# Causal attention and routed experts on one core: transposes in 64-row halves, shared columns for diagonal blocks, one ring of PSUM banks

## The chip, the core and the metric

The kernel runs on one core of a Trainium2 chip. The metric is the device time of one execution in microseconds; the time before is the median of three runs. Engines: TensorE (PE; its weight loads are listed as PEld), VectorE (DVE), ScalarE (ACT), GpSimd (POOL), and SyncE (SP), whose queue issues most DMA transfers.

## What is computed

A causal attention over 4 sequences of 448 tokens with 12 heads of 64, then a layer of 8 experts, each of which takes its 224 best tokens in one greedy order over all (token, expert) scores.

```python
def _attn_ref(q, k, v):                       # (4, 12, 448, 64)
    scores = scale * np.matmul(q, k.transpose(0, 1, 3, 2))
    scores = np.where(mask, -1000000000.0, scores)   # mask: above the diagonal
    scores = scores - np.max(scores, axis=-1, keepdims=True)
    attn = np.exp(scores)
    attn = attn / (np.sum(attn, axis=-1, keepdims=True) + 1e-09)
    return np.matmul(attn, v)

def _moe_ref(x, w_gate, w1, w2):              # x: (1792, 768), 8 experts
    order = np.argsort(-(x @ w_gate).flatten())
    ...                                       # a token goes to its first expert that still has room (224)
    for e in range(E):
        h = np.maximum(x[assigned == e] @ w1[e], 0.0)
        out[assigned == e] = h @ w2[e]
```

## The kernel before

The kernel has two stages. Attention (class Attention, the first 164 us or so) works on 24 pairs of heads; a pair's two heads sit in the lower and the upper 64 partitions. Routing and experts (classes Router and Experts) follow. In each stage a planner (class Schedule) puts every operation in order at build time: each operation is a task with an engine, a guessed duration, dependencies and a priority, and the planner walks through time and lets each engine take the ready task of highest priority. Some copies may go to ScalarE or VectorE, whichever the planner finds free. TensorE is the exception: its tasks hang on one another in the order in which they are added (`pe`, line 454).

That order is set in `plan` (line 434). In turn n TensorE does the scores of pair n in two sets (query blocks 2 and 3, then 1 and 0), the values of pair n-2, the transposes of P of pair n-1, the rows of pair n-3, and, when a set of four pairs is complete, the logits.

A pair goes through these steps. `scores` multiplies the four query blocks of 128 rows (the first and last 64 tokens share one block) with as many keys as the mask leaves (QM: 192, 320, 448 and 64 columns), each head in its own half of the array's rows and in its own PSUM bank. `mask` (VectorE) adds the mask and finds the row maximum, `exp` (ScalarE) writes the exponentials to a tile P and their sums. `transp` turns the 16 blocks of P of 128 x 128, one instruction each, four to a bank: groups 0 and 1 hold one head's blocks, group 2 blocks of both, group 3 the diagonal blocks of 64 keys, each of which holds both heads' in its two halves. `keep_pt` copies them to the tile PT: groups 0 and 1 with 512 columns on ScalarE, group 2 with 512 columns on either engine, group 3 as two copies of 64 partitions x 256 columns, one for each head. PT has a half for each head; the places that the causal mask leaves empty were set to zero once at the start. `av` multiplies four key blocks of V (448, 320, 192 and 64 query columns) with it, each head in its own half of the array's columns, and `xt_ev` evicts the result. For the first 12 pairs (LATE) `rows_tr` and `rows_dve` turn the result back to token rows and scale it by the sums; the later pairs' rows are turned after attention.

PSUM has eight banks. Four belong to the ring "s" (scores), four to the ring "t" (everything else): the dependency `ring(name, n)` makes a task wait until the bank that it will write has been emptied.

Of the kernel before, what the change touches and what calls it, by code (L numbers as in the profile page):

```python
# [30 lines left out]
KO = (256, 704, 64, 0)  # L31
KM = (448, 320, 192, 64)
XO = (0, 64, 192, 320)
LATE = 12
# [126 lines left out]
class Attention(Schedule):  # L161
    def __init__(self, ctx, tc, gc, keep, k, qk, vP, wgP, xd, L):
# [17 lines left out]
        t = self.ps.tile([P, 512], F32, name="t", bufs=4)  # L180
# [14 lines left out]
        self.PTs = [self.cs.tile([P, 2, 1024], F32, name=f"PT{z}") for z in range(2)]  # L195
        for t in self.PTs:
            for sd, o in ((sd, o) for sd in range(2) for o in (0, 640)):
                nc.gpsimd.memset(t[64 - 64 * sd:128 - 64 * sd, sd, o:o + 128], 0.0)


# [17 lines left out]
    def load_v(self, g):  # L218
        v = self.ld.tile([P, 4, NC, D], F32, name="v")
        b, h = divmod(4 * g, H)  # L220
        self.nc.sync.dma_start(v, self.vP[:, b, h:h + 4])
        for u in range(4):
            self.V[4 * g + u] = v[:, u]

    def scores(self, pp, lst):
        ts = [self.ps.tile([P, 512], F32, name="s", bufs=4) for _ in range(2)]
# [53 lines left out]
    def keep_pt(self, e, pp, c):  # L280
        PT = self.PTs[pp % 2]
        if c < 2:
            self.copy(e, PT[:, c, 128:640], self.T[pp, c])
        elif c == 2:
            self.copy(e, PT[:, :, 768:], self.T[pp, 2].rearrange("p (s k) -> p s k", s=2))
        else:
            sd = c - 3
            h = slice(64 * sd, 64 * sd + 64)
            self.copy(e, PT.rearrange("p s (c z k) -> p s c z k", z=2, k=64)[h, sd, 0:6:5],
                      self.T[pp, 3][h].rearrange("p (c z y k) -> p c z y k", c=2, z=2, y=2)[:, :, :, 1])  # L290
# [65 lines left out]
    def logits_mm(self, p0, m):  # L356
        t = self.ps.tile([128, S], F32, name="t", bufs=4)
# [4 lines left out]
    def logits_direct(self, pp):  # L362
        b, q = divmod(pp, 6)
        if q == 4:
            self.u[pp] = self.ps.tile([P, NC, 128], F32, name="t", bufs=4)
# [9 lines left out]
    def logits_tr(self, p0, m):  # L375
        u = self.u[p0] = self.ps.tile([P, NC, 128], F32, name="t", bufs=4)
# [33 lines left out]
    def ring(self, name, n):  # L410
        r = self.rings.setdefault(name, [])
        return r[-n] if len(r) >= n else []

    def plan(self, rt):
        add = self.add
        self.rings = {}
# [41 lines left out]
    def score_set(self, pp, lst):  # L458
# [11 lines left out]
        a = self.pe(m * 4 / 2400.0 + 0.01 * len(lst), work, [self.got[pp]] + self.ring("s", 2), 1)  # L470
        free = []
        for sd in range(2):
            for i in lst:
# [5 lines left out]
        self.rings.setdefault("s", []).append(free)  # L479
# [4 lines left out]
    def turns(self, pp):  # L484
# [3 lines left out]
        every = [(sd, i) for sd in range(2) for i in range(NC)]  # L488
# [844 lines left out]
```

## Time and profile before

| | before |
|---|---|
| median of three runs | 486.27 us (484.93 to 487.37) |
| profiled execution | 486.56 us, span 484.9 us |
| instructions | 10216 |
| TensorE busy | 471.2 us (97%) |
| TensorE weight loads | 398.3 us (82%) |
| VectorE busy | 376.7 us (78%) |
| ScalarE busy | 298.9 us (62%) |
| granted TensorE clock, mean | 0.999 |

The shares are means over a stage of attention and a stage of experts that have different limits, so the windows by stage have to be read beside them. A matmul's end is modelled and matmuls overlap in the pipeline: the step from one start to the next is what one costs, not its listed duration. Of an fp32 product each instruction of the program is two loads and two matmuls in the trace; a transpose is one of each.

### The profile page before, as it was taken

Reading aid. Unit: us, or ns where it says so; the run is one execution under the profiler, and the core shown is the slowest. Engines: PE = TensorE matmul, PEld = TensorE weight load, DVE = VectorE, ACT = ScalarE, POOL = GpSimd, SP = SyncE. Lnnn points to the kernel's source line nnn. Section 1 sums busy time; section 2 is a strip of 40 time slices with the busy share of each in tenths; the row PEclk is TensorE's granted clock in tenths of the full one; section 3 lists DMA queues with packets and bytes.
Section 4 is the critical chain, followed back from the end, with each engine's and each line's share of the span. In section 5 each row is a group of like instructions: output and inputs, shape, how many; then the busy total and the mean of one; then the engine's idle time right before and its main releaser. Section 6 shows DMA issues by size and latency. Waiting matters only on the chain.

```text
span 484.9 us, 10216 instructions
## 1 busy us (share of the span) xinstructions
PE 471.2 (97%) x3697; PEld 398.3 (82%) x3697; DVE 376.7 (78%) x1316; ACT 298.9 (62%) x759; POOL 52.6 (11%) x100
## 2 busy tenths in 40 slices
PE   8999999999999898999989999999999999999994
PEld 4767777676766767998979999989899989999994
DVE  4988788897788675799989999999999585684510
ACT  4997988889989542345654664572763673764410
POOL 7000000000000110100310300300114110301001
PEclk9999999999999999999999999999999999999999
DMA  8633183172000078497577677764955886681101
GB/s 288 268 120 120 44 310 120 45 263 91 1 2 2 23 236 286 142 334 245 181 248 258 198 215 243 245 193 134 321 197 183 315 271 216 220 245 64 53 1 57
DMA packets 19187, 84.84 MB, mean 175 GB/s; under 512 B 2240, under 2 KB 4928, under 8 KB 19136
## 3 DMA queue, kind: packets, MB, share of 16 engines
q1 hardware_dynamic: 16464, 73.14, 44.5%
q0 software_dynamic: 2672, 11.04, 7.3%
q8 instruction: 29, 0.48, 0.4%
q14 instruction: 22, 0.18, 0.1%
HBM read 73.16 MB, written 11.01 MB: 174 GB/s over the span
## 4 chain that ended last, share of the span: by engine, by line
PE 77%; DVE 11%; ACT 5%; DMA 4%; issue 2%; POOL 1%; POOLq 0%; DVEq 0%; ACTq 0%
PE po L1258 23%; PE ph L1224 10%; PE s L233 9%; PE t L297 9%; PE t L268 8%; PE ph L1228 5%; DVE wl L1154 4%; PE ph L1219 3%; ACT P L254 3%; DMA xio<-xd,idx 2%; DVE G L697 2%; PE ph L1189 2%; PE rt L798 2%; DMA out<-xio,idx 1%; PE po L1219 1%
## 5 line engine op out<-in xcount | busy, mean ns | idle before, releaser
L1154 DVE TENSOR_TENSOR wl<-wr,wh 128x512 fp32r<-128x512 f32 x180 | 116.2, 682 | 13.5 <-ACT wh L1148 13.5
L1148 ACT CAST wh<-wr 128x1536 fp32r<-128x1536 f32 x60 | 88.9, 1482 | 59.9 <-DMA wr<-in_w 38.8
L1224 PE MATMUL ph<-xhl,wh 128*128 128x448 f32 x336 | 109.2, 380 | 0.0
L254 ACT ACTIVATE P<-Sm,mx 128x448 f32<-128x448 f32 (+2 forms) x192 | 95.7, 504 | 19.9 <-DVE mx L244 19.8
L1228 PE MATMUL ph<-xhl,wl 128*128 128x224 f32 x336 | 88.8, 264 | 0.0
L1258 PE MATMUL po<-wh,HH 128*112 128x384 f32 x256 | 68.2, 342 | 0.0
L1258 PE MATMUL po<-wh,HL 128*112 128x384 f32 x256 | 67.9, 341 | 0.0
L1258 PE MATMUL po<-wl,HH 128*112 128x384 f32 x256 | 67.3, 339 | 0.0
L1224 PEld LDWEIGHTS ph<-xhl,wh 128*128 128x128 f32 x336 | 63.1, 188 | 5.1 <-issue 0.6
L1228 PEld LDWEIGHTS ph<-xhl,wl 128*128 128x128 f32 x336 | 64.1, 191 | 0.0
L233 PE MATMUL s<-raw 64*128 64x448 f32 (+3 forms) x384 | 51.8, 404 | 0.3 <-DVE mx L244 0.2
L233 PEld LDWEIGHTS s<-raw 64*128 64x128 f32 x384 | 31.9, 187 | 20.7 <-issue 15.7
L268 PE MATMUL t<-idf,P 128*128 128x128 f32 x384 | 47.7, 277 | 0.0
L297 PE MATMUL t<-PT,v 128*64 128x448 f32 (+3 forms) x384 | 46.8, 386 | 0.0
L297 PEld LDWEIGHTS t<-PT,v 128*64 128x64 f32 x384 | 25.4, 136 | 23.8 <-issue 14.0
L1258 PEld LDWEIGHTS po<-wl,HH 128*112 128x112 f32 x256 | 44.0, 175 | 0.3
L268 PEld LDWEIGHTS t<-idf,P 128*128 128x128 f32 x384 | 41.5, 140 | 2.3 <-ACT P L254 0.4
L1258 PEld LDWEIGHTS po<-wh,HL 128*112 128x112 f32 x256 | 43.2, 175 | 0.3
L1258 PEld LDWEIGHTS po<-wh,HH 128*112 128x112 f32 x256 | 43.1, 175 | 0.3
L274 DVE COPY PT<-t 64x256 f32<-64x256 f32 (+1 forms) x56 | 29.6, 529 | 16.3 <-PE t L268 10.5
L244 DVE CUSTOM_DVE_ANT_0 Sm<-s,MK 128x448 f32<-128x448 f32 (+2 forms) x72 | 33.2, 486 | 9.5 <-PE s L233 8.8
L244 DVE CUSTOM_DVE_ANT_0 Sm<-s,MR 128x64 f32<-128x64 f32 (+3 forms) x120 | 40.5, 380 | 0.0
(170 smaller groups left out, 617.1 us busy)
## 6 DMA issues: line engine op xcount, KB each, us to landing
wr<-in_w SPq DMA_DIRECT2D x64, 768.0 KB, 5.1
raw<-in_qk SPq DMA_DIRECT2D x11, 896.0 KB, 8.9
v<-in_v SPq DMA_DIRECT2D x12, 512.0 KB, 4.5
xd<-xio SPq DMA_DIRECT2D x2, 1152.0 KB, 5.0
xd<-xio SPq DMA_DIRECT2D x3, 576.0 KB, 4.3
xd<-xio SPq DMA_DIRECT2D x3, 192.0 KB, 5.2
raw<-in_qk SPq DMA_DIRECT2D x1, 448.0 KB, 4.3
xd<-xio SPq DMA_DIRECT2D x1, 384.0 KB, 4.2
```

The source lines that it names most:

```text
L233: self.nc.tensor.matmul(ts[sd][:, o:o + m], q[:, 0, QS[i]:QS[i] + P], k, start=True, stop=True)
L244: self.nc.vector.tensor_tensor_reduce(Sm[:, QO[i] + sd * m:QO[i] + sd * m + m], self.S.pop((pp, sd, i)), mk, -0.125, 3.0e38, OP.add, OP.mi ...
L254: self.nc.scalar.activation(X[:, s], Sm[:, s], AF.Exp, bias=mx[:, sd, i:i + 1], scale=-1.0, accum_out=self.RS[b][:, pr, sd * NC + i:sd * N ...
L268: self.nc.tensor.transpose(t[:, n * P:n * P + P], X[:, o:o + P], idf)
L274: self.nc.vector.tensor_copy(out, x)
L297: self.nc.tensor.matmul(self.AV[pp][sd * 64:sd * 64 + 64, XO[j]:XO[j] + KM[j]], self.V[2 * pp + sd][:, j, :], self.PTs[pp % 2][:, sd, KO[j ...
L1148: self.nc.scalar.copy(hi, self.R[p, c])
L1154: self.nc.vector.tensor_sub(lo[:, s], self.R[p, c][:, s], hi[:, s].bitcast(F32))
L1219: nc.tensor.matmul(t[:, c], self.R[p, f // 2][:, s], self.X[0, 0][:, d, 0, c], start=d == 0, stop=d == 5)
L1224: nc.tensor.matmul(t[:, :2 * CAP], hi[:, s], x[:, d].rearrange("p z t -> p (z t)"), start=d == 0, stop=False)
L1228: nc.tensor.matmul(t[:, :CAP], lo[:, s], x[:, d, 0], start=False, stop=d == 5)
L1258: self.nc.tensor.matmul(self.T[p, "o", u][z][:, :384], a[p][:, f, u * C:u * C + C], w[:, o:o + 384], start=f == 0 and n == 0, stop=f == 7 ...
```

## The change

A block of P is now turned as two halves of 64 rows: 64 x 128 weights from the lower or the upper partitions against a 64 x 64 identity. The lower half goes to one bank, the upper half to another, side by side in 64 columns each. The copies to PT (`keep_pt(e, pp, g, z)`) put them together again with a target of 64-element runs. Of the four diagonal blocks only the upper halves are turned, and the two heads share their columns in PT: V gets three more blocks per head (7 instead of 4), padded with zeros in the half that belongs to the other head, and `av` does seven products a head instead of four, over 384, 256, 128 and four times 64 columns. PT is an ordinary tile of 2048 columns with two buffers, and nothing in it is set to zero beforehand. The rows of the first 12 pairs are turned two pairs at a time, in halves as well, into two banks, and scaled with one operation for each head (`rows_two`). All banks of attention come from one ring of eight in the order of their use (`bank`, `room`). The planner's guesses change with it: scores, transposes and rows count as one mode.

```diff
-KO = (256, 704, 64, 0)
-KM = (448, 320, 192, 64)
-XO = (0, 64, 192, 320)
+KR = (384, 256, 128)
+DJ = (2, 1, 3, 0)
...
+    def bank(self):
+        return self.ps.tile([P, 512], F32, name="s", bufs=8)
...
-        v = self.ld.tile([P, 4, NC, D], F32, name="v")
+        v = self.ld.tile([P, 4, 2 * NC - 1, D], F32, name="v")
...
     def transp(self, pp, g):
-        t = self.T[pp, g] = self.ps.tile([P, 512], F32, name="t", bufs=4)
-        if g < 2:
-            parts = [(g, 2, 2)] + [(g, i, 0) for i in range(3)]
-        elif g == 2:
-            parts = [(sd, i, 1) for sd in range(2) for i in (1, 2)]
+        t = self.T[pp, g] = [self.bank() for _ in range(2)]
+        if g == 0:
+            parts = [(sd, i, j) for sd in range(2) for i, j in ((0, 0), (1, 0), (2, 0), (2, 2))]
         else:
-            parts = [(None, i, 0) for i in (2, 1, 3, 0)]
+            parts = [(sd, i, 1) for sd in range(2) for i in (1, 2)] + [(None, i, 0) for i in DJ]
         for n, (sd, i, j) in enumerate(parts):
             o = QO[i] + (QM[i] - 64 if sd is None else QM[i] + 64 + (i - j) * P if sd else j * P)
-            self.nc.tensor.transpose(t[:, n * P:n * P + P], X[:, o:o + P], idf)
+            for z in range(sd is None, 2):
+                h = slice(64 * z, 64 * z + 64)
+                self.nc.tensor.transpose(t[z][:, n * 64:n * 64 + 64], X[h, o:o + P], idf[h, h])
...
+    def keep_pt(self, e, pp, g, z):
+        if pp not in self.PT:
+            self.PT[pp] = self.wk.tile([P, 2048], F32, name="PT", bufs=2)
+        n = 256 if g > z else 512
+        x = self.PT[pp][:, g * 1024:g * 1024 + 2 * n].rearrange("p (c z k) -> p c z k", z=2, k=64)[:, :, z]
+        self.copy(e, x, self.T[pp, g][z][:, :n].rearrange("p (c k) -> p c k", k=64))
 
     def av(self, pp, js):
         if 0 in js:
-            self.AV[pp] = self.ps.tile([P, 512], F32, name="t", bufs=4)
+            self.AV[pp] = self.bank()
+        PT = self.PT[pp]
         for j in js:
             for sd in range(2):
-                self.nc.tensor.matmul(self.AV[pp][sd * 64:sd * 64 + 64, XO[j]:XO[j] + KM[j]], self.V[2 * pp + sd][:, j, :],
-                                      self.PTs[pp % 2][:, sd, KO[j]:KO[j] + KM[j]], start=j == 0, stop=j == 3)
+                v = self.V[2 * pp + sd]
+                o = (512 * sd, 1024 + 256 * sd, 512 * sd + 384)[j] if j < 3 else 1600 + 128 * (j - 3)
+                w, m = (384 - KR[j], KR[j]) if j < 3 else ((320, 192, 384, 64)[j - 3], 64)
+                self.nc.tensor.matmul(self.AV[pp][sd * 64:sd * 64 + 64, w:w + m],
+                                      v[:, j if j < 3 else 3 + (3, 2, 0, 1)[j - 3], :], PT[:, o:o + m],
+                                      start=j == 0, stop=j == 6)
...
     def rows_tr(self, pp):
-        self.T[pp] = self.ps.tile([P, 512], F32, name="t", bufs=4)
-        self.rows_mm(pp, self.T[pp])
+        self.T[pp] = [self.bank() for _ in range(2)]
+        for u, i, sd in ((u, i, sd) for u in range(2) for i in range(NC) for sd in range(2)):
+            h = slice(64 * sd, 64 * sd + 64)
+            o = u * 256 + i * 64
+            self.nc.tensor.transpose(self.T[pp][sd][:, o:o + 64], self.block(self.XT[pp - 1 + u][h], i), self.k["idf"][h, h])
...
-    def ring(self, name, n):
-        r = self.rings.setdefault(name, [])
-        return r[-n] if len(r) >= n else []
+    def room(self, n):
+        o = len(self.ring) - 8
+        return sum(self.ring[max(o, 0):max(o + n, 0)], [])
...
-        for g, need in ((3, every), (0, every), (1, every), (2, every)):
-            a = self.pe(0.44, lambda g=g: self.transp(pp, g), [self.exps[pp, sd, i] for sd, i in need] + self.ring("t", 4))
...
+        for g in range(2):
+            a = self.pe(0.51, lambda g=g: self.transp(pp, g), every + self.room(2), 1)
+            for z in range(2):
+                dur = {"DVE": 0.6, "ACT": 0.47} if g <= z else {"DVE": 0.35, "ACT": 0.29}
+                c = self.add("ACT" if g == 0 else "ACT/DVE", dur["ACT"] if g == 0 else dur,
+                             lambda e="ACT", g=g, z=z: self.keep_pt(e, pp, g, z), [a] + self.avs[-2:-1], pr + 0.3)
+                self.pts[pp, g, z] = c
+                self.ring.append([c])
...
-        for js, cs in (((0,), (0, 1, 3, 4)), ((1, 2, 3), (2,))):
+        for js, g in (((0, 2), 0), ((1, 3, 4, 5, 6), 1)):
```

## Rows read from the trace of the kernel before

**Rows 1.** Windows by stage: busy us (instructions) of each engine, PEclk, DMA share, GB/s.
```profile
8.00:26.00 18.00, 17.68 (x134) 12.28 (x134) 16.01 (x82) 17.96 (x67) 2.26 (x9) 1.00 0.76 288
26.00:104.80 78.80, 78.79 (x659) 55.62 (x658) 65.99 (x278) 68.06 (x234) 0.45 (x3) 1.00 0.37 131
104.80:148.20 43.40, 43.40 (x363) 29.83 (x362) 35.74 (x154) 40.03 (x139) 0.00 (x0) 1.00 0.18 65
148.20:164.00 15.80, 15.34 (x130) 10.54 (x130) 11.39 (x52) 9.73 (x32) 1.76 (x4) 1.00 0.01 2
```

**Rows 2.** Chain of waits in order of time: start, us, what; attention.
```profile
26.01 2.04 PE s L233 x16
...
52.14 0.44 PE t L324 x4
...
104.81 2.04 PE s L233 x16
106.85 1.88 PE t L297 x16
108.73 1.90 PE t L268 x16
...
148.17 2.04 PE s L233 x16
```

**Rows 3.** Groups by form, 26 to 104.8 us (count, busy, mean ns, idle); last 8 to 26.
```profile
L254 ACT ACTIVATE P<-Sm,mx 128x448 f32<-128x448 f32 x24 | 15.9, 662 | 10.2 <-DVE mx L244 10.2
L272 ACT COPY PT<-t 128x512 f32<-128x512 f32 x24 | 12.9, 583 | 0.0
L274 DVE COPY PT<-t 64x256 f32<-64x256 f32 x18 | 7.6, 423 | 5.7 <-PE t L268 2.8 <-ACT PT L272 2.8
L272 ACT COPY PT<-t 64x256 f32<-64x256 f32 x6 | 2.2, 365 | 0.2
...
L272 ACT COPY PT<-t 64x256 f32<-64x256 f32 x4 | 1.4, 358 | 0.0
```

**Rows 4.** Weight loads of one pair's transposes: timeline at 96 us, group of the page.
```profile
96.15 1.73 PEld L268 LDWEIGHTS t<-idf,P 128*128 128x128 f32 x16
...
L268 PEld LDWEIGHTS t<-idf,P 128*128 128x128 f32 x384 | 41.5, 140 | 2.3 <-ACT P L254 0.4
```

**Rows 5.** Four transposes of 64 rows: timeline at 158.7 us, min/median/max of line 378.
```profile
158.73 0.33 PEld L378 LDWEIGHTS t<-idf,lt 64*128 64x128 f32 x4 [0.17 <-issue]
158.73 0.46 PE L378 MATMUL t<-idf,lt 64*128 64x64 f32 x4
...
L378 PEld LDWEIGHTS t<-idf,lt x24: 137/140/142, 45.6 to 158.9; 128*128 128x128 f32 x20, 64*128 64x128 f32 x4
L378 PE MATMUL t<-idf,lt x24: 222/273/275, 45.7 to 159.0; 128*128 128x128 f32 x20, 64*128 64x64 f32 x4
```

**Rows 6.** Scores, two heads in two row halves: timeline at 99 us, group by form.
```profile
98.92 0.30 PEld L233 LDWEIGHTS s<-raw 64*128 64x128 f32 x4 [0.17 <-issue]
99.41 0.19 PEld L233 LDWEIGHTS s<-raw 64*128 64x128 f32 x2 [0.18 <-issue]
...
100.70 0.33 PE L233 MATMUL s<-raw 64*128 64x192 f32 x2
...
L233 PE MATMUL s<-raw 64*128 64x192 f32 x48 | 5.9, 322 | 0.0
```

**Rows 7.** Window of the early count, line 726 alone: PE, PEld, PEclk, DMA, GB/s.
```profile
163.64:163.89 0.25, 0.25 (x10) 0.25 (x10) 1.00 0.00 0
```

**Rows 8.** Values in 64 columns: timeline at 102.6 us, groups by form.
```profile
102.63 0.28 PE L297 MATMUL t<-PT,v 128*64 128x64 f32 x4
...
L297 PEld LDWEIGHTS t<-PT,v 128*64 128x64 f32 x192 | 12.7, 136 | 11.7 <-issue 6.9 <-ACT P L254 1.1 <-DVE mx L244 0.2
...
L297 PE MATMUL t<-PT,v 128*64 128x64 f32 x48 | 3.4, 220 | 0.0
```

**Rows 9.** Timeline of TensorE at 13 us: end of pair 0's transposes, scores of pair 2.
```profile
13.09 0.38 PE L268 MATMUL t<-idf,P 128*128 128x128 f32 x2
13.40 0.65 PE L233 MATMUL s<-raw 64*128 64x448 f32 x2
```

More of the change, by code (lines that the diff above doesn't have):

```diff
@@ L179, in __init__ @@
         nc.vector.memset(zero, 0.0)
[L180 removed]
+        t = self.bank()
         for _ in range(WARM):
@@ L225, in scores @@
     def scores(self, pp, lst):
-        ts = [self.ps.tile([P, 512], F32, name="s", bufs=4) for _ in range(2)]
+        ts = [self.bank() for _ in range(2)]
         o = 0
@@ L468, in work @@
                 self.fire(self.qfree[pp])
-        a = self.pe(m * 4 / 2400.0 + 0.01 * len(lst), work, [self.got[pp]] + self.ring("s", 2), 1)
-        free = []
+        a = self.pe(m * 4 / 2400.0 + 0.01 * len(lst), work, [self.got[pp]] + self.room(2), 1)
         for sd in range(2):
+            free = []
             for i in lst:
@@ L478, in score_set @@
                                            [d], pr + early)
-        self.rings.setdefault("s", []).append(free)
+            self.ring.append(free)
         if last:
@@ L487, in turns @@
         pr = 5.5 - 0.1 * pp
-        every = [(sd, i) for sd in range(2) for i in range(NC)]
-        for g, need in ((3, every), (0, every), (1, every), (2, every)):
-            a = self.pe(0.44, lambda g=g: self.transp(pp, g), [self.exps[pp, sd, i] for sd, i in need] + self.ring("t", 4))
-            last = [a]
-            for c in (3, 4) if g == 3 else (g,):
-                dur = {"DVE": 0.61, "ACT": 0.49} if c < 3 else {"DVE": 0.35, "ACT": 0.27}
-                one = c < 2
-                up = 0.6 if c > 2 else 0.3
-                last = [self.add("ACT" if one else "ACT/DVE", dur["ACT"] if one else dur,
-                                 lambda e="ACT", c=c: self.keep_pt(e, pp, c), last + self.ring("av", 2), pr + up)]
-                self.pts[pp, c] = last[0]
-            self.rings.setdefault("t", []).append(last)
+        every = [self.exps[pp, sd, i] for sd in range(2) for i in range(NC)]
+        for g in range(2):
[6 more added lines that the diff above has]
+                self.ring.append([c])
     def values(self, pp):
@@ L504, in values @@
         pr = 5.5 - 0.1 * pp
-        for js, cs in (((0,), (0, 1, 3, 4)), ((1, 2, 3), (2,))):
-            m = sum(KM[j] for j in js)
+        for js, g in (((0, 2), 0), ((1, 3, 4, 5, 6), 1)):
+            m = sum((384, 256, 128, 64, 64, 64, 64)[j] for j in js)
             def work(js=js):
                 self.av(pp, js)
-                if 2 in js and pp in self.vfree:
+                if 1 in js and pp in self.vfree:
                     self.fire(self.vfree[pp])
-            deps = [self.pts[pp, c] for c in cs] + [self.gotv[pp // 2]]
-            a = self.pe(m * 4 / 2400.0 + 0.02, work, deps + (self.ring("t", 4) if 0 in js else []), 2)
-        self.rings.setdefault("av", []).append([a])
+            deps = [self.pts[pp, g, z] for z in range(2)] + [self.gotv[pp // 2]]
+            a = self.pe(m * 4 / 2400.0 + 0.02, work, deps + (self.room(1) if 0 in js else []), 2)
+        self.avs.append(a)
         def ev(e):
@@ L531, in rows_at @@
         pr = 5.3 - 0.1 * pp
[L532 to L535 removed]
+        t = self.pe(0.5, lambda: self.rows_tr(pp), [self.xts[pp]] + self.room(2), 1)
+        for sd in range(2):
+            d = self.add("DVE", 0.62, lambda sd=sd: self.rows_two(pp, sd), [t, self.rec[pp]], pr + 0.3)
+            self.ring.append([d])
+            self.done_x.append(d)
         if b < LATE // 6:
@@ L544, in logits @@
         if pp in (NP - 2, NP - 1):
-            free = self.ring("t", 4) if q == 4 else []
+            free = self.room(1) if q == 4 else []
             self.lts = self.pe(0.4, lambda: self.logits_direct(pp), [self.xts[pp]] + free)
             if q == 4:
-                self.rings.setdefault("t", []).append([self.event(0.0)])
+                self.ring.append([])
             return
```

51 lines of the change are left out of this document (20 added, 31 removed).

## Prediction

> **What bounds the kernel now.** I read the stage windows first [rows 1]. From 26 us to 148 us TensorE is busy in 78.79 of 78.80 us and 43.40 of 43.40 us, ScalarE in 86% and 92%, VectorE in 84% and 82%, at a granted clock of 1.00. From 8 to 26 us it is the other way round: ScalarE is busy in 17.96 of 18.00 us. The chain of waits [rows 2] says the same: from 26.01 us it runs through TensorE alone, sixteen scores, sixteen value matmuls, sixteen transposes, then scores again, with nothing between. So inside the attention stage a pair of heads costs what TensorE needs for it: (104.81 - 26.01)/12 = 6.57 us while rows are turned in the stage, (148.17 - 104.81)/7 = 6.19 us after that, made of 2.04 + 1.88 + 1.90, rows 0.44, and a rest of some 0.35 that is logits, once in four pairs. From 148.2 us the tail of the last two pairs runs to about 164 us; what follows is routing and experts, which the change doesn't touch, so what attention saves comes off the end one for one. The groups by form [rows 3] price each operation of the stage; ScalarE's 10.2 us of idle there are waits for masks, that is, for scores that TensorE delivers late.
>
> **The change part by part, TensorE.** Transposes of P: 16 instructions of 128 rows become 28 of 64 rows. They come as 12 pairs (lower and upper half of a block, into two banks) and 4 upper halves alone, so 16 steps if the two of a pair run together. Price now: 16 loads in 1.73 us of which the last takes 0.14, so 15 steps of 0.106 [rows 4]; the chain charges 1.90 for all, up to the next scores [rows 2]. Price of a step with 64 rows and 64 columns: the kernel has four such transposes, alone, in its second to last logits set: four loads in 0.33 us with a last of 0.14, three steps of 0.063; four matmuls in 0.46 with a last of 0.22, 0.24 for three steps, so 0.05 more at the entry [rows 5]. New price 16 x 0.063 + 0.05 = 1.06, a saving of 0.84 a pair.
>
> That a pair runs in one step isn't shown for transposes, but the scores are the same shape of work (64 x 128 weights in either half of the rows, two banks): two loads take 0.19 us from the first one's start to the last one's end and four 0.30, so two and two start together, 0.11 apart; two matmuls of 0.322 are over in 0.33 [rows 6]. Bounds for 28 instructions: 12 + 4 steps of 0.063 (1.06), or 28 steps of 0.063 one after the other (1.81). I take the first, since the row of the scores is the nearest. Issuing doesn't limit it: ten small matmuls, each with its load, begin within 0.25 us, 0.028 apart [rows 7], and a step here has two such pairs in 0.063.
>
> For a rule against it: the Trainium skill, "TensorE: Matmul & The Clock Gate", section "LDWEIGHTS (loading the stationary operand)", says that a load's time goes by its columns, at P/1.2 ns, however few rows it fills, so that half the rows cost as much as all, 107 ns for 128 columns. By that the 28 loads would take 28 x 0.107 = 3.0 us if they followed one another. The 0.063 of [rows 5] are 128 columns in less than that, so the trace does not agree.
>
> Rows: four transposes a pair (0.44) become sixteen halves for two pairs, 8 steps x 0.063 = 0.50, 0.25 a pair: -0.19 in the pairs with rows. Scores: their first loads now come 0.17 us late behind the 128-row transposes [rows 6]. After transposes of the same 64-row shape that wait should go, except in the one pair of four where a logits matmul lies between; part of it is already in the 1.90, so I take -0.08 (between 0 and -0.17). Values: 16 instructions become 28, with the same 1024 columns a head; four blocks of 64 stand where one of 448 and one of 64 gave 512. A 64-column step takes 0.06 [rows 8] (four in 0.28, a last of 0.22), eight are 0.48, and 512 columns at the present rate (1.88/2048 of a column pass) are 0.47: +0.02. Upper bound, if the load of 0.136 [rows 8] isn't hidden behind a 64-column pass: 8 x 0.076 = +0.6.
>
> Sum: 6.57 - 0.84 - 0.19 - 0.08 + 0.02 = 5.48 us with rows, 6.19 - 0.84 - 0.08 + 0.02 = 5.29 without.
>
> **VectorE and ScalarE, the cover that is gone.** They now work 65.99 + 68.06 = 134.05 us in twelve pairs, 11.17 a pair, and 35.74 + 40.03 in seven, 10.82 [rows 1]. The change takes away the two 64 x 256 copies of a pair (7.6 + 2.2 us in twelve pairs, 0.82 a pair) and puts one 128 x 256 copy there, whose length along the free axis is that of one of them, 0.42 on VectorE, 0.36 on ScalarE [rows 3]: -0.41. The three 512-column copies stay, two tied to ScalarE as before; their target in runs of 64 elements I cost at nothing (no copy of before has such a target; at worst it adds what a second instruction adds over one of half the length: two copies of 256 columns take 2 x 0.36 for ScalarE's 0.58 in one, +0.14 each, 0.2 us a pair for either engine). Rows on VectorE: two of 512 columns for two pairs, as now. So 10.76 and 10.41 a pair: 5.38 and 5.21 for each engine if the planner could share perfectly. That is level with TensorE's 5.48 and 5.29. All three engines would reach their limit at once, so I don't expect TensorE's whole gain to show.
>
> The Trainium skill, "TensorEngine Tiling (Array Packing)", section "PSUM Bottleneck", says that splitting the array speeds TensorE and not the emptying of PSUM, which may become the limit. Here the busy sums of [rows 1] bear it out at 5.4 us a pair.
>
> How near do two engines come to full? From 8 to 26 us, when TensorE didn't hold them back, they worked 16.01 + 17.96 of 36 us, 94% [rows 1]. I take 10.76/2/0.944 = 5.70 and 10.41/2/0.944 = 5.51 us a pair; bounds are TensorE's 5.48 and 5.29, and 88% (today's mean of 85 to 87% a little bettered), 6.1 and 5.9.
>
> **What else moves.** Start: ScalarE bounds it, and four of its copies of 64 x 256 (1.4 us in 8 to 26 [rows 3]) become at most two to four of 128 x 256 that VectorE may take: -0.8. Tail (148.2 to 164): two more blocks of transposes, each 0.84 shorter [rows 2]: -1.7. Loads: each v transfer grows from 512 to 896 KB. The first one stands ahead of the queries and keys of pairs 2 and 3 on SyncE's queue; 384 KB at the 288 GB/s of 8 to 26 us [rows 1] delay those by 1.3 us. Pair 2's scores start at 13.40 [rows 9], behind transposes and not behind a load, and ScalarE is at work without a gap then; so I take 0, at most 1.3. Later loads have four buffers of lead. The zeroing of the old PT tiles on GpSimd goes, at nothing either way.
>
> Ring: 8 banks in one order instead of 4 + 4, with the same 10.5 banks a pair. A bank of scores must now be emptied before a later transpose can write, and after a rows step the first scores of a pair need the last masks of the pair before, the second ones the copies of its first transposes. Behind such a scores matmul on TensorE stand the values and transposes, and behind its result the masks and exponentials. Cost 0 if VectorE does the masks before other work and the copies leave at once; otherwise it is the second rival below.
>
> **Sum of the forecast**: 12 x (6.57 - 5.70) = 10.4, 7 x (6.19 - 5.51) = 4.8, 0.8, 1.7: 17.7 us. The profiled execution took 486.56 us (span 484.9), 0.3 above the median of the three runs, 486.27. So 469.
>
> **Rivals.**
> A, TensorE's whole gain is had: 12 x 1.09 + 7 x 0.90 + 2.5 = 21.9, 464 to 465. For it: the shares are close. Against: three engines that share a pair through strict orders, where even now two idle 8 to 18%.
> B, the ring and the copies take the place of the transposes: a copy of the first transposes waits behind one exponential (0.66) and then takes two times 0.58, so the second scores, due 1.0 us into a pair, would start up to 0.6 late in pairs with rows, half that in others: 5.48 + 0.6 = 6.1 and 5.29 + 0.3 = 5.6 to 5.85 us, some 10.5 saved in all, about 476, and with copies behind two exponentials 480.
> C, the two halves of a pair run one after the other at 0.063: turns 1.81, rows 0.50 a pair: 6.57 - 0.09 + 0.06 - 0.08 + 0.02 = 6.48 and 6.04; 1.1 + 1.0 + 0.8 + 0.2 = 3.1 saved, 483.5.
> D, slower: the halves run one after the other and each costs a whole step, about 0.109, as a 128-row transpose does (the chain's 1.90 over 16 less the entry [rows 2]). Place: the transposes of P and rows. Turns 28 x 0.109 = 3.05 (+1.15 in 24 pairs), rows 1.74 for two pairs (+0.86 six times), scores -0.08 x 24: +27.6 + 5.2 - 1.9 = +31, 517. It decides from (1.90 + 0.08)/28 = 0.071 an instruction on, and [rows 5] show 0.063. The rule of the Trainium skill cited above ("TensorE: Matmul & The Clock Gate", loads) gives this same end.
> E, the gain is lost later (constants for routing that VectorE does in its free time slip behind attention, the values' loads aren't hidden): 484 to 488.
>
> **How the numbers follow.** Forecast (88 to 98% of the two engines, 465 to 476) 0.64; A 0.08 (462 to 465); B beyond 476 0.12; C 0.05; D 0.05; E 0.06. The range 462 to 480 leaves out C, D, E and a little of A and B, under 2 in 10. About 0.5% (2.4 us) is what a measurement of this kernel can tell from no change. Faster: forecast, A, B and most of C, 0.87. Same: E's better part and a rest of C, 0.06. Slower: D and E's rest, 0.07.
>
> **What would show it.** Transposes right: TensorE's sixteen-step block in about 1.06 us with two loads starting together; wrong: starts 0.06 or 0.11 apart for every instruction. Bound right: in the window of the twelve pairs ScalarE and VectorE over 92% busy, TensorE at 92 to 97%, a chain of waits that goes through exponentials and PT copies; A if TensorE is still without a gap; B if scores wait for PT copies or masks for over 0.3 us a pair. Tail and experts: the same length after the last values. The prediction is wrong if pairs stay over 6.1 us, or if a lower granted clock shows in the stage.

## The result and the profile after

The changed kernel takes 469.35 us (median of four runs, 468.12 to 472.33) against 485.71 of the kernel before on the same chip: a ratio of 0.9668, 95% interval 0.9613 to 0.9722. On a second chip it took 469.6, ratio 0.9676 (0.9606 to 0.9747). The forecast was 469.0, the range 462 to 480.

| | after |
|---|---|
| median of four runs | 469.35 us (468.12 to 472.33) |
| profiled execution | 468.12 us, span 466.4 us |
| instructions | 11432 |
| TensorE busy | 450.0 us (96%) |
| TensorE weight loads | 392.9 us (84%) |
| VectorE busy | 367.6 us (79%) |
| ScalarE busy | 292.4 us (63%) |
| granted TensorE clock, mean | 0.995 |

First the windows by stage, after (columns as in [rows 1]: PE, PEld, DVE, ACT, POOL busy, clock, DMA share, GB/s). The second is the stage with rows, the third the pairs without, the fourth the tail.

```profile
8.00:26.00 18.00, 16.12 (x226) 12.97 (x222) 16.34 (x87) 18.00 (x68) 0.77 (x8) 1.00 1.02 407
26.00:95.00 69.00, 68.78 (x1018) 52.54 (x1017) 62.93 (x279) 66.08 (x235) 0.46 (x3) 1.00 0.52 184
95.00:135.00 40.00, 39.67 (x548) 29.11 (x544) 33.52 (x159) 39.22 (x137) 0.00 (x0) 1.00 0.21 78
135.00:150.00 15.00, 12.58 (x161) 9.86 (x158) 11.12 (x47) 9.69 (x41) 1.76 (x4) 1.00 0.03 12
```

The twelve pairs that needed 78.8 us [rows 1] need 69. TensorE is still all but gapless (68.78 of 69.00), and ScalarE has risen from 86% to 96%, VectorE from 84% to 91%, so none of the three has much room left. In the first window ScalarE is the one at work without a gap, as before.

Where the time went is read from the starts of the pairs' first scores (line 230 after, 233 before). After, from TensorE's timeline:

```profile
21.82 0.64 PE L230 MATMUL s<-raw 64*128 64x448 f32 x1
...
90.25 0.64 PE L230 MATMUL s<-raw 64*128 64x448 f32 x1
...
129.38 0.65 PE L230 MATMUL s<-raw 64*128 64x448 f32 x2
```

These are pairs 4, 16 and 23: (90.25 - 21.82)/12 = 5.70 us a pair, then (129.38 - 90.25)/7 = 5.59. The two profiles of the kernel after against the one of before, in us:

| stretch | before | after, 1st chip | after, 2nd chip | forecast of the saving |
|---|---|---|---|---|
| start of pair 4 | 25.94 | 21.82 | 24.51 | 0.8 |
| a pair, 4 to 16 (12) | 6.567 | 5.703 | 5.673 | 12 x 0.87 = 10.4 |
| a pair, 16 to 23 (7) | 6.195 | 5.589 | 5.588 | 7 x 0.68 = 4.8 |
| pair 23's scores to the last values' end | 13.98 | 13.35 | 14.79 | 1.7 |
| the rest, routing and experts | 322.78 | 323.68 | 320.58 | 0 |
| span | 484.86 | 466.42 | 467.08 | 17.7 |

The nineteen pairs give 14.6 and 15.0 us, against 15.2 forecast. Start, tail and rest differ by 1.4 to 3.1 us between the two profiles of one kernel, in good part because the granted clock fell to 0.50 in different places (the last two sections say where and what it cost), so a single profile says little of a term of 1 us there. In the nineteen pairs the clock is 1.00 in both. Of the 4.1 us at the first chip's start, 0.8 is chance: the first scores of all began at 4.87 there, on the second chip at 5.68, before at 5.66.

The chain of waits, after (start, us, what; line 293 is values, 265 the turns of P, 328 rows, 385 the turns of the logits):

```profile
33.87 2.04 PE s L230 x16
35.91 1.91 PE s L293 x28
37.82 0.96 PE s L265 x25
...
38.96 0.50 PE s L328 x12
39.45 0.59 PE s L385 x4
...
84.27 1.02 DVE PT L271 x2
85.29 0.60 DVE xio L335
...
88.86 1.75 ACT P L251 x6
90.61 0.95 ACT PT L269 x2
...
129.45 2.04 PE s L230 x16
...
133.44 0.53 ACT xt L269
133.97 0.66 ACT P L251 x2
134.63 0.96 ACT PT L269 x2
```

It runs through TensorE, as before [rows 2], up to 84 us; then through VectorE's PT copies and row scalings and ScalarE's exponentials and PT copies up to 98; through TensorE again to 133, through ScalarE to 139, and at the end through TensorE. From 84.3 to 97.4 us TensorE works on without a gap beside that chain, which makes it wait only at the end of the stretch. The 1.90 of sixteen turns is now 0.96, with three of the 28 left over among the rows that follow.

### The profile page after: what moved, and what is told of

Same layout as the page of the kernel before. It is cut to its first block, busy times and chain, and to the rows that moved or that the text cites. A ratio compares the mean times of both kernels' runs of the same rounds, so it can differ in the third digit from the quotient of the medians.

```text
span 466.4 us, 11432 instructions
## 1 busy us (share of the span) xinstructions
PE 450.0 (96%) x4321; PEld 392.9 (84%) x4321; DVE 367.6 (79%) x1305; ACT 292.4 (63%) x746; POOL 51.9 (11%) x92
## 4 chain that ended last, share of the span: by engine, by line
PE 70%; DVE 13%; ACT 8%; DMA 4%; issue 2%; POOL 1%; POOLq 0%; DVEq 0%; ACTq 0%
PE po L1264 24%; PE ph L1230 11%; PE s L293 7%; PE s L230 7%; ACT P L251 5%; PE ph L1234 5%; PE s L265 4%; DVE wl L1160 4%; DMA xio<-xd,idx 3%; PE ph L1195 2%; DVE G L703 2%; PE ph L1225 2%; PE po L1225 2%; PE rt L804 1%; ACT PT L269 1%
## 5 line engine op out<-in xcount | busy, mean ns | idle before, releaser
L1160 DVE TENSOR_TENSOR wl<-wr,wh 128x512 fp32r<-128x512 f32 x180 | 116.2, 683 | 13.7 <-ACT wh L1154 13.7
L230 PE MATMUL s<-raw 64*128 64x64 f32 (+3 forms) x384 | 52.4, 400 | 0.0
L230 PEld LDWEIGHTS s<-raw 64*128 64x128 f32 x384 | 39.4, 187 | 11.3 <-issue 8.6
L293 PE MATMUL s<-PT,v 128*64 128x64 f32 (+3 forms) x672 | 47.5, 293 | 0.7 <-ACT PT L269 0.6
L293 PEld LDWEIGHTS s<-PT,v 128*64 128x64 f32 x672 | 32.1, 137 | 18.7 <-issue 10.8
L251 ACT ACTIVATION_READ_ACCUMULATOR P<-Sm,mx 128x1 f32 x192 | 40.0, 208 | 0.0
L1240 ACT ACTIVATE HH<-hs 128x224 fp32r<-128x224 f32 x56 | 21.9, 392 | 25.6 <-DVE hs L1248 24.5
L1248 DVE TENSOR_TENSOR hs<-ph,hc 128x224 f32<-128x224 f32 x56 | 21.7, 388 | 19.1 <-ACT hc L1244 16.1
```

What stands on the lines that cost most here:

```text
L230: self.nc.tensor.matmul(ts[sd][:, o:o + m], q[:, 0, QS[i]:QS[i] + P], k, start=True, stop=True)
L251: self.nc.scalar.activation(X[:, s], Sm[:, s], AF.Exp, bias=mx[:, sd, i:i + 1], scale=-1.0, accum_out=self.RS[b][:, pr, sd * NC + i:sd * N ...
L293: self.nc.tensor.matmul(self.AV[pp][sd * 64:sd * 64 + 64, w:w + m], v[:, j if j < 3 else 3 + (3, 2, 0, 1)[j - 3], :], PT[:, o:o + m], star ...
L1160: self.nc.vector.tensor_sub(lo[:, s], self.R[p, c][:, s], hi[:, s].bitcast(F32))
L1240: self.nc.scalar.activation(self.HH[p][:, f], self.P[p, f][:, :CAP], AF.Relu)
L1248: self.nc.vector.tensor_tensor(t, self.P[p, f][:, :CAP], self.Hc.pop((p, f)), op=OP.add)
```

## Experiments

The theories were these. TensorE alone: the shorter turns carry the whole gain, and only what lengthens TensorE's order costs time. The copying engines alone: the copy saved on ScalarE and VectorE carries it. All three: each is at its limit, and any work added to one of them costs nearly its price. And of the ring and the order of the halves: what they are worth by themselves.

**Whole blocks again, all else kept.** Blocks of P are turned with 128 rows, copies are contiguous; the ring, the shared columns of the diagonal blocks, the longer values and the rows in halves stay. The planner's guess for a turn is set to match.

```diff
-            for z in range(sd is None, 2):
-                h = slice(64 * z, 64 * z + 64)
-                self.nc.tensor.transpose(t[z][:, n * 64:n * 64 + 64], X[h, o:o + P], idf[h, h])
+            self.nc.tensor.transpose(t[n // 4][:, n % 4 * P:n % 4 * P + P], X[:, o:o + P], idf)
...
```

> The changed kernel with one part undone: P is turned in 16 blocks of 128 rows again (eight banks in one ring, the saved copy, the shared diagonal columns and the rows in halves stay). Theory 1 (the gain is TensorE's: halves in pairs at 0.062 us a step instead of 0.109): turns go from about 1.0 to 1.9 us in 24 pairs, and TensorE bounds the stage alone again: +18 to +20 us, 487 to 489 us, that is, the whole gain is gone although the copy that was saved stays saved. Theory 2 (the saved copy and the shorter work of ScalarE and VectorE carry the gain): at most +5 us, 470 to 474 us.

Measured: 483.92 us, ratio to before 0.9944 (0.9919 to 0.9969); 6.50 us a pair with rows, 6.22 without. Its window by stage, and its chain of waits over one pair:

```profile
26.00:95.00 69.00, 69.00 (x762) 50.56 (x759) 53.10 (x233) 61.00 (x216) 0.30 (x2) 1.00 0.43 161
```

```profile
45.15 2.04 PE s L230 x16
47.19 1.91 PE s L292 x28
```

TensorE has no gap, and VectorE is back to 77%, ScalarE to 88%. The saved copy is still saved here and brings little by itself, since TensorE bounds the pair alone: all that is left of the change comes to some 2.7 us. That is below the 487 to 489 expected of the first theory, which had the whole gain go, and far above the 470 to 474 of the second. The halves carry 0.80 and 0.64 us a pair, 14.3 to 14.6 us of the 16.4 between the medians. The values cost 1.91 with 28 instructions against 1.88 with 16, as forecast (+0.02).

**Rows with 128 rows again.**

```diff
-            self.nc.tensor.transpose(self.T[pp][sd][:, o:o + 64], self.block(self.XT[pp - 1 + u][h], i), self.k["idf"][h, h])
+        for u in range(2):
+            self.rows_mm(pp - 1 + u, self.T[pp][u])
...
```

> The changed kernel with the rows of the first 12 pairs turned in blocks of 128 rows again, two pairs at a time. TensorE's price: 8 steps of 0.109 instead of 8 of 0.062 and one change of shape more (about 0.15 us), 0.5 us in six places. Theory 1 (TensorE bounds the pairs with rows): +3 us, 472 to 473 us. Theory 2 (ScalarE and VectorE bound them): 0 to +1 us, 469 to 470 us.

Measured: 470.64 us, ratio 0.9661 (0.9604 to 0.9719), not to be told from the kernel after by its time. In the trace 5.89 us a pair with rows, 0.19 to 0.22 more, and 5.55 without. The rows' halves are worth some 0.2 us in each of twelve pairs, nearly what they take off TensorE; the gain is too small beside the scatter of start and tail to show in the median, which lies between the two expectations.

**A fourth copy of 256 columns**, on whichever engine is free, its result not used.

```diff
+    def again(self, e, pp):
+        self.copy(e, self.wk.tile([P, 256], F32, name="again", bufs=2), self.T[pp, 1][0][:, :256])
...
-                self.ring.append([c])
+                more = []
+                if g > z:
+                    more = [self.add("ACT/DVE", dur, lambda e: self.again(e, pp), [a], pr + 0.3)]
+                self.ring.append([c] + more)
```

> The changed kernel with one more copy of 128 x 256 out of PSUM in each pair, on whichever of ScalarE and VectorE the planner chooses (0.36 or 0.42 us of work, result unused). Theory 1 (TensorE alone bounds the stage): 0 to +1 us, 469 to 470 us. Theory 2 (ScalarE and VectorE bound it at 94% of both): 0.41/2/0.94 = 0.22 us in 24 pairs, +5 us, 474 to 475 us. Theory 3 (all three at their limit at once, as forecast): between, +2 to +4 us, 471 to 473 us.

**Four pairs of halves turned twice**, 0.25 us of TensorE a pair.

```diff
-        for n, (sd, i, j) in enumerate(parts):
+        for n, (sd, i, j) in list(enumerate(parts))[:4 * g] + list(enumerate(parts)):
...
-            a = self.pe(0.51, lambda g=g: self.transp(pp, g), every + self.room(2), 1)
+            a = self.pe(0.51 + 0.25 * g, lambda g=g: self.transp(pp, g), every + self.room(2), 1)
```

> The changed kernel with four steps of paired half transposes more in each pair (the same blocks into the same places again, 0.25 us of TensorE). Theory 1 (TensorE alone): 24 x 0.25 = +6 us, 475 to 476 us. Theory 2 (ScalarE and VectorE): 0 to +1 us, 469 to 470 us. Theory 3 (all three): between, +3 to +5 us, 472 to 474 us.

Measured, the copy: 471.66 us, ratio 0.9698 (0.9654 to 0.9742); 5.99 us a pair with rows (+0.29 to 0.32), 5.58 without (0). The turns: 473.44, ratio 0.9725 (0.9676 to 0.9774); 5.90 with rows (+0.20 to 0.23), 5.72 without (+0.13). The windows by stage of the two, in this order:

```profile
26.00:95.00 69.00, 68.02 (x955) 50.45 (x954) 61.52 (x270) 64.08 (x228) 0.45 (x3) 1.00 0.47 173
```

```profile
26.00:95.00 69.00, 69.00 (x1060) 53.03 (x1058) 59.09 (x260) 64.17 (x226) 0.45 (x3) 1.00 0.44 162
```

In pairs with rows either addition costs time. The copy's 0.29 to 0.32 is more than the half of its 0.41 that two engines sharing it evenly would make of it. With it TensorE gets gaps (0.98 us of 69), and its scores wait for ScalarE's PT copies; with the turns it has no gap. The wait in the run with the copy (the columns are explained at the two rings below):

```profile
PEld s L230 <- ACT PT L269: 1.2, 4, 0.5
```

For TensorE alone the copy would have been free, for the copying engines alone the turns. So with rows neither is the limit by itself: TensorE sets the pace, and the other two are so near that one copy more makes it wait. (This edit also holds a bank until the added copy is done; the profile names nothing that waited for that copy, but its share isn't separated.) Without rows the copy is free against the kernel after, and the turns show 0.13. That kernel has one wait of 0.8 us among these pairs; against the 5.47 us that they take without it, in the run with free copies below, the turns cost their whole 0.25. Medians differ from the kernel after's by 2 to 4 us, with intervals that overlap; the per-pair times carry this verdict.

**Two rings of four banks, as before the change.** Scores from one, everything else from the other.

```diff
-    def bank(self):
-        return self.ps.tile([P, 512], F32, name="s", bufs=8)
+    def bank(self, name="t"):
+        return self.ps.tile([P, 512], F32, name=name, bufs=4)
...
-    def room(self, n):
-        o = len(self.ring) - 8
-        return sum(self.ring[max(o, 0):max(o + n, 0)], [])
+    def room(self, n, ring=None):
+        ring = self.ring if ring is None else ring
+        o = len(ring) - 4
+        return sum(ring[max(o, 0):max(o + n, 0)], [])
...
```

> The changed kernel with two rings of four banks again (scores in one, everything else in the other), all else as it is. Theory 1 (the one ring is needed, since turns now take two banks at a time and rows two more): the rows must wait for the copies of the transposes just made, and the transposes for the eviction of the values, 0.5 to 1 us in some twelve places: +5 to +10 us, 474 to 480 us. Theory 2 (the second rival of the forecast, the one ring makes scores wait for the copies and costs time): faster, 466 to 468 us. Theory 3 (the ring doesn't matter): 469 to 470 us.

**The kernel before with one ring of eight** (its transposes and copies untouched).

```diff
-        t = self.ps.tile([P, 512], F32, name="t", bufs=4)
+        t = self.ps.tile([P, 512], F32, name="s", bufs=8)
...
-        return r[-n] if len(r) >= n else []
...
+        r = self.rings.setdefault("s", [])
+        o = len(r) - 8
+        return sum(r[max(o, 0):max(o + (2 if name == "s" else 1), 0)], [])
...
```

> The kernel before with one part of the change alone: one ring of eight banks instead of two of four. Theory 1 (there TensorE has no gap, so that banks aren't what it waits for): no change, ratio 0.997 to 1.003. Theory 2 (the ring is a gain by itself): 1 to 3 us faster. Theory 3 (its one order is a loss by itself): 1 to 3 us slower.

Measured: two rings in the kernel after, 477.94 us, ratio 0.983 (0.9772 to 0.9887), 6.26 us a pair with rows and 5.87 without. One ring in the kernel before, 486.9, ratio 0.9996 (0.9957 to 1.0034), 6.55 and 6.19. The window of the first, and its waits from 26 to 95 us (engine, what it waited to do <- what ended the wait: us in all, times, longest):

```profile
26.00:95.00 69.00, 66.27 (x921) 48.17 (x919) 56.45 (x248) 62.42 (x218) 0.30 (x2) 1.00 0.45 160
```

```profile
DVE xio L335 <- PE t L328: 3.1, 6, 0.7
...
PEld t L328 <- ACT PT L269: 2.1, 4, 0.8
PE t L328 <- ACT PT L269: 1.6, 4, 0.6
PEld s L230 <- DVE PT L271: 1.5, 2, 0.7
```

With four banks for everything but scores, the rows (line 328) wait for ScalarE's PT copies to empty a bank, and VectorE's row scalings wait in turn for them; TensorE has 2.7 us of gaps in the window. The new turns fill two banks at a time and the rows two more. So the ring alone gives nothing where TensorE is slow, and some 8 us of the change's 16 hang on it once the turns are short. Gains of parts don't add up here: the halves without the ring give about half, the ring without the halves nothing.

**All lower halves of a task first, then all upper ones.**

```diff
-        for n, (sd, i, j) in enumerate(parts):
-            o = QO[i] + (QM[i] - 64 if sd is None else QM[i] + 64 + (i - j) * P if sd else j * P)
-            for z in range(sd is None, 2):
+        for z in range(2):
+            for n, (sd, i, j) in enumerate(parts):
+                if sd is None and z == 0:
+                    continue
+                o = QO[i] + (QM[i] - 64 if sd is None else QM[i] + 64 + (i - j) * P if sd else j * P)
```

> The changed kernel with the same 28 half transposes of a pair in another order on TensorE: in each of the two groups first all lower halves, then all upper ones, instead of lower and upper in turn. Theory 1 (each half of the array's rows takes its own next instruction, as the trace shows at the end of the turns, where a later step's lower half begins while upper halves are still to come): 0 to +1 us, 469 to 471 us. Theory 2 (only neighbours in the program run together): 28 steps of 0.062 instead of 16, +0.74 us in the 20 or so pairs that TensorE bounds, +13 to +16 us, 482 to 485 us.

Measured: 475.14 us, ratio 0.978 (0.9695 to 0.9865); 5.93 and 5.78 us a pair. TensorE's timeline of one pair's turns (line 267 here), in whole and cut at 59.12 us, and what comes next:

```profile
58.83 1.51 PE L267 MATMUL s<-idf,P 64*128 64x64 f32 x28
...
58.83 0.46 PE L267 MATMUL s<-idf,P 64*128 64x64 f32 x4
...
60.27 0.58 PE L368 MATMUL s<-xt,WG 128*32 128x448 f32 x4
```

The kernel after, ahead of the same kind of work:

```profile
54.54 1.07 PEld L265 LDWEIGHTS s<-idf,P 64*128 64x128 f32 x28
54.55 1.21 PE L265 MATMUL s<-idf,P 64*128 64x64 f32 x28
...
55.68 0.58 PE L366 MATMUL s<-xt,WG 128*32 128x448 f32 x4
```

In turn about, 28 turns last 55.68 - 54.55 = 1.13 us; lower first, 60.27 - 58.83 = 1.44. One after the other they would be 28 x 0.062 = 1.74 at least, all paired 1.13. In the first task of eight and eight the first upper half starts with the fifth lower one: four lower ones alone by 59.12. So here an instruction for the free half ran ahead by about four places, not by eight. The turns are 0.31 us longer, and 0.23 to 0.26 us a pair with rows are lost, 0.19 without. Both plain answers, strictly in order and wholly free, were wrong.

**Every PT copy on whichever engine is free.** The two first ones were tied to ScalarE.

```diff
-                c = self.add("ACT" if g == 0 else "ACT/DVE", dur["ACT"] if g == 0 else dur,
-                             lambda e="ACT", g=g, z=z: self.keep_pt(e, pp, g, z), [a] + self.avs[-2:-1], pr + 0.3)
+                c = self.add("ACT/DVE", dur,
+                             lambda e, g=g, z=z: self.keep_pt(e, pp, g, z), [a] + self.avs[-2:-1], pr + 0.3)
```

> The changed kernel with the first two copies of PT free to go to VectorE as well, as the planner finds it idle (now they are tied to ScalarE). Theory 1 (all three engines are at their limit, and the shares are already level): -1 to +1 us, 468 to 471 us. Theory 2 (ScalarE alone is the limit beside TensorE, as its 66 of 69 us in the twelve pairs with rows hint): -3 to -5 us, 464 to 466 us.

**The kernel after once more**, on the same chip.

> The changed kernel once more, on the same chip as the three others and beside the same runs of the kernel before: 469 to 471 us. In its first profile the first scores began at 4.87 us, where the kernel before and four variants began at 5.6 to 5.7; if that is chance, they begin at 5.6 to 5.7 here and the profiled execution is 0.8 us longer.

Measured: 466.98 us, ratio 0.9622 (0.9553 to 0.9691), and for the kernel after 469.6, 0.9676 (0.9606 to 0.9747). Their windows, free copies first:

```profile
26.00:95.00 69.00, 68.53 (x1000) 51.24 (x998) 65.23 (x279) 62.69 (x226) 0.45 (x3) 1.00 0.50 179
```

```profile
26.00:95.00 69.00, 68.94 (x1006) 52.62 (x1004) 62.54 (x278) 65.99 (x234) 0.45 (x3) 1.00 0.50 182
```

Some 3 us of work move from ScalarE to VectorE, and the pairs take 5.74 with rows (against 5.67 to 5.70) and 5.47 without (against 5.59). Where VectorE had room, without rows, 0.11 us a pair are gained, all of it in one place (see the pairs without rows below); with rows, where TensorE sets the pace, nothing is. The median is 2.6 us lower, between the two expectations, but the intervals overlap. The kernel after came out as expected: its first scores began at 5.68, so the early start of its first profile was chance, and the profiled execution was 0.66 us longer.

Two runs on top of this one. The first gives the planner guesses for the masks nearer to their durations, the second gives it a later landing of the experts' first gathers, so that it puts other work ahead of what waits for them.

```diff
-                d = add("DVE", (0.355, 0.49, 0.62, 0.225)[i], lambda sd=sd, i=i: self.mask(pp, sd, i), [a], pr + 0.25 + early)
+                d = add("DVE", (0.28, 0.41, 0.545, 0.145)[i], lambda sd=sd, i=i: self.mask(pp, sd, i), [a], pr + 0.25 + early)
```

> The kernel with free copies (e7) and, besides, the planner's guesses for the masks set to the steps that the trace shows (0.28, 0.41, 0.545 and 0.145 us instead of 0.355, 0.49, 0.62 and 0.225), so that it no longer takes VectorE for fuller than it is; the work is the same. Theory 1 (the stage is at the limit of three engines, so that only the share between them can move): -2 to +1 us against e7, 465 to 468 us. Theory 2 (the planner's order is what holds the stage back): -4 us or more, 463 us or less.

```diff
-            x.append(add("DMA", 0.96, lambda: None, [a], 9.0, (1.0, 2.0)[u] if p == 0 else 6.5 if p == 1 else 5.0))
+            x.append(add("DMA", 0.96, lambda: None, [a], 9.0, (2.0, 2.5)[u] if p == 0 else 6.5 if p == 1 else 5.0))
```

> The kernel with free copies (e7) and a longer guess for the first gather of the experts' rows (2.0 and 2.5 us instead of 1.0 and 2.0), so that the planner puts more filler matmuls between routing and the first expert. In the first profile of the changed kernel TensorE stood still for some 2.3 us there and the granted clock was 0.50 in the two us after it, 1.3 us lost. Theory 1 (the fillers hold the clock): no stretch below 1.00 there, -1 to 0 us in the median, 465.5 to 467 us. Theory 2 (the guess only shifts the order): 0 to +1 us.

Measured: 466.72 us, ratio 0.9573 (0.9521 to 0.9626), and 468.97, ratio 0.965 (0.9572 to 0.9728). Pairs take 5.69 and 5.47 with the first, 5.73 and 5.47 with the second. The masks' guesses change nothing beyond the free copies; the later landing brings no gain: its median is 2.0 us above that of the free copies alone, outside both expectations, though the intervals overlap. Its theory on the clock isn't settled: its profile has no stretch below 1.00 behind the first gather, but neither has that of the free copies alone, nor the second of the kernel after. The free copies, alone or with the guesses, have the lowest medians of all, below both kernels, though only by about 0.5% below the one after.

## Why the prediction was right

That the halves shorten the turns, and by how much, came out as forecast, and the range holds the result. What sets the pair was half right, and several terms missed by more than their sum did.

**The turns.** Sixteen steps of two halves together were forecast, 1.06 us; measured 1.13 ahead of work of another shape, with loads of a pair starting together and 0.062 from step to step (28 loads in 1.07 us). Ahead of rows or scores, which also use 64 rows, the four single upper halves at the end share their time with the lower halves of the next block. The first two loads of the turns of P (265), then these turns and the rows (328), in the timeline after:

```profile
60.52 0.14 PEld L265 LDWEIGHTS s<-idf,P 64*128 64x128 f32 x2
...
60.52 1.02 PE L265 MATMUL s<-idf,P 64*128 64x64 f32 x25
61.32 0.28 PE L328 MATMUL s<-idf,xt 64*128 64x64 f32 x1
61.38 0.22 PE L265 MATMUL s<-idf,P 64*128 64x64 f32 x1
61.44 0.22 PE L328 MATMUL s<-idf,xt 64*128 64x64 f32 x1
```

The rows begin 0.80 us after the turns, before the last turns do. With that rivals C (one after the other at 0.063) and D (at 0.109, the slower case) fall, and with D the rule of the Trainium skill ("TensorE: Matmul & The Clock Gate", "LDWEIGHTS (loading the stationary operand)") that a load costs by its columns alone. The 28 loads would have taken 3.0 us by its figure one after the other, or 1.7 in sixteen steps, both estimates from that page; they took 1.07.

**The term of TensorE's sum that was mis-sized.** It was 5.48 us with rows. In the second profile four pairs in a row, from 24.51 to 47.03, pass without a gap of TensorE, 22.52/4 = 5.63 a pair; the next four take 22.77:

```profile
24.51 0.64 PE L230 MATMUL s<-raw 64*128 64x448 f32 x1
...
47.03 0.64 PE L230 MATMUL s<-raw 64*128 64x448 f32 x1
...
69.80 0.64 PE L230 MATMUL s<-raw 64*128 64x448 f32 x1
```

In the first profile the four between 33.80 and 56.57 us, less one wait of 0.25, give the same 22.52. What was not counted is the change of shape that remains where 64-row work meets 128-row work: the logits' four turns cost 0.59 instead of 0.44, the turns ahead of logits 1.13 instead of 1.06, turns and rows together 1.64 (0.96 + 0.18 + 0.50) instead of 1.06 + 0.50 = 1.56. The scores, too, stand behind the logits' 128-row work in two pairs of four, not in one as forecast, and cost 2.04 there as before. With the rows turned by 128 again, the logits' turns behind them are back at 0.44:

```profile
65.11 1.02 PE s L321 x8
66.13 0.44 PE s L383 x4
```

Rival A needed 5.48, so its 464 to 465 was out of reach whatever the other engines did.

**What sets the pair.** The forecast took VectorE and ScalarE at 94.4% of two engines, so 5.70; measured (62.93 + 66.08)/138 = 93.5%, and 5.70 and 5.67 a pair. The -0.41 for the copies is right: a 128 x 256 copy takes 411 ns, a strided 512-column one 598 on ScalarE, against 423 and 583 [rows 3]. The groups by form, 26 to 95 us (count, busy, mean ns, idle):

```profile
L269 ACT COPY PT<-s 128x512 f32<-128x512 f32 x32 | 16.7, 598 | 0.0
...
L271 DVE COPY PT<-s 128x256 f32<-128x256 f32 x12 | 4.9, 411 | 0.7 <-PE s L265 0.5
```

But the step as written, that the two engines set the pair and TensorE has 3 to 8% to spare, does not hold. TensorE is busy for 99.7% of the window, which was the forecast's sign of rival A, and the chain leaves it for some 11 of the 69 us only. It sets the pair at 5.63; on top come 0.04 to 0.07, above all one wait of 0.25 in four pairs, of the turns for ScalarE's exponentials. TensorE's waits on its scores and turns from 26 to 95 us in the first profile:

```profile
PEld s L230 <- issue: 4.9, 18, 0.7
...
PEld s L265 <- ACT P L251: 0.6, 3, 0.3
```

The runs with longer turns agree: four pairs take 23.5 us with 0.25 added a pair, 23.7 in the other order (+0.31), against 22.5. So of the 0.22 us by which a pair lies above 5.48, 0.15 is TensorE's own and 0.07 at most the others', to whom the forecast had given all of it. That the number came out all the same is luck in this part: the two engines' term lay a little above what TensorE really needs. That they are near enough to matter, as forecast, the run with the added copy shows. That emptying PSUM may become the limit once the array is split, as the Trainium skill says ("TensorEngine Tiling (Array Packing)", "PSUM Bottleneck"), the trace bears out in part: with rows a copy of 0.41 us more, for either engine, costs 0.3 a pair; without rows it costs nothing.

**Pairs without rows** came to 5.59 instead of 5.51, 0.5 us in all. TensorE sets these too, at 5.47 (5.29 forecast): six of the seven take within 0.02 us what they take with free copies, where TensorE is busy for 40.00 of 40 us. The other, pair 17, takes 6.98 us against 6.17:

```profile
95.19 0.64 PE L230 MATMUL s<-raw 64*128 64x448 f32 x1
...
97.81 1.98 PE L293 MATMUL s<-PT,v 128*64 128x384 f32 x28 [0.33 <-ACT PT L269]
...
102.17 0.65 PE L230 MATMUL s<-raw 64*128 64x448 f32 x2
```

Its values wait for PT copies on ScalarE, which is 98% busy there (39.22 of 40; VectorE 84%), and its logits take 0.4 longer. The forecast shared the work evenly, but the two copies tied to ScalarE prevent it; with the tie gone the wait is gone.

**The ring.** Cost 0 was forecast with rival B at 476 to 480. No scores wait for masks or copies for 0.3 us a pair in the kernel after; B falls. With two rings a wait of that kind does appear, on the rows more than on the scores, and gives 478. That the one ring was needed for the gain, the forecast had not said.

**Start, tail, rest.** The start gave 4.1 and 1.4 us instead of 0.8. Without the chance of the first scores the first is 3.3; in the second, pair 2 took 6.58 us, 3.4 of them at a clock of 0.50, against 4.93 in the first; if the clock made these 1.65, it would be 3.1. With whole blocks the way from the first scores to pair 4 takes 19.32 us, in the kernel before 20.28, in the first profile after 16.95: most of this gain is the halves', which the forecast left out there because ScalarE bounds the start. The tail gave 0.6 and -0.8 instead of 1.7. The last values took 3.41 us at 0.50 in the second profile and 1.98 in the first, which is the whole difference. The tail's term took TensorE as its bound, and there the chain goes through ScalarE's exponentials and copies from 133 to 139 us. The larger values' loads cost nothing, as taken: pair 2's scores begin right behind the work ahead of them on TensorE. Rival E falls: nothing that attention saved came back later beyond 0.9 us in one profile, where 1.3 were lost at 0.50, and the other has 2.2 us the other way.

So the total is nearer than its terms: the start was 2.3 to 2.5 too low, the tail 1.1 too high, and what was lost at half clock, some 1.3 and 3.1 us, stood in no term. That these nearly cancel is luck. The forecast named a lower granted clock in the stage as a sign of being wrong; it shows in the second profile, at the start and in the tail, but not in the nineteen pairs.

## What to carry to other kernels

When one engine is relieved, add up the others per unit of work before forecasting, changes of shape included: here TensorE came out at 5.63 us a pair instead of 5.48, and the other two so near that one copy more made it wait, so the gain was about three quarters of what the shorter instructions alone promised (16.4 of 21.9 us). Turns with 64 rows pay where lower and upper halves stand in turn about in the program, with banks enough that both may be written at once. A resource that gives nothing by itself (the ring in the kernel before) can carry half the gain of the step that it enables, so undo parts from the finished change as well as adding them one by one.

## What the runs showed of the hardware

The two row halves of TensorE run on by themselves, but not without limit: lower halves of the next block start before upper halves that stand ahead of them in the program (61.32 against 61.38 us above), and with eight lower halves in a row the first upper one starts with the fifth.

The granted clock fell to 0.50, 1.2 of 2.4 GHz, for some 3.4 us at different places in the two profiles of one kernel: in the first after at about 168 us, in the second at 13.7 and at 143.4. The windows, in this order, and the last values of attention (293), which fall into the third:

```profile
168.00:170.00 2.00, 2.00 (x11) 2.00 (x11) 0.00 (x0) 0.00 (x0) 0.00 (x0) 0.50 1.02 424
```

```profile
13.70:17.10 3.40, 3.40 (x17) 2.66 (x15) 2.98 (x16) 3.40 (x14) 0.00 (x0) 0.50 1.02 422
143.40:146.80 3.40, 3.09 (x28) 2.04 (x24) 0.26 (x1) 0.27 (x1) 0.24 (x1) 0.50 0.00 0
```

```profile
143.08 3.41 PE L293 MATMUL s<-PT,v 128*64 128x384 f32 x28
```

In the first profile the drop followed the wait for the first gather (160.95 to 166.36 us, TensorE busy for 3.67 of 5.41), and sixteen matmuls of the first expert took 3.34 us, against 2.04 in the kernel before. In the second profile TensorE was busy for 3.69 of 5.30 us in the same place (from 164.70), and no drop followed: 2.04. From 8 to 12 us, ahead of the drop at 13.7, TensorE was busy for 2.66 of 4 us, before the change for 3.78; but in the first profile after it was 2.23, and no drop followed there. So how busy TensorE was just before does not tell these places apart. Drops come with both kernels: the recorded runs of the kernel after have mean clocks of 0.985 to 0.995, those of the kernel before 0.986 to 0.999. What decides where a drop falls stays open.
